# One head group's V on SyncE's queue in fp32, and the third keys in a buffer of raw keys: an attention and feed-forward kernel on one core

## The chip, the cores and the metric

The kernel runs on 1 core of one Trainium2 chip. The metric is device time in microseconds (us) of one execution; lower is better. TensorE (PE) multiplies matrices, VectorE (DVE) and ScalarE (ACT) work element by element, GpSimd (POOL) and SyncE (SP) here almost only issue DMAs. A DMA that POOL issues may change the type on its way (fp32 in HBM, fp16 in SBUF); POOL's transfers are the queue q0 of the profile ("software_dynamic"), SP's are q1 ("hardware_dynamic"). Both are moved by the same 16 DMA engines.

## What is computed

```
scores = scale * np.matmul(q, k.transpose(0, 1, 3, 2))      # q, k, v: 8 x 12 x 448 x 64, fp32
scores = scores - np.max(scores, axis=-1, keepdims=True)
attn = np.exp(scores)
attn = attn / (np.sum(attn, axis=-1, keepdims=True) + 1e-09)
attn_out = np.matmul(attn, v).astype(np.float32)

x = np.ascontiguousarray(attn_out.transpose(0, 2, 1, 3)).reshape(B * S, H * D)   # 3584 x 768
h = x @ w_in                                                # 768 x 2048
g = h * (1.0 / (1.0 + np.exp(-h)))
out = (g @ w_out).astype(np.float32)                        # 2048 x 768
```

Everything is read in fp32 and computed in fp16 with fp32 sums in PSUM.

## The kernel before

**Tiling.** A unit is one batch and one group of four heads (hg); there are 8 x 3 = 24 of them, numbered n = 3 x batch + hg. For each unit the raw keys and queries (128 partitions, 896 fp16 columns, 224 KB) are loaded, turned with 32 x 32 transposes on DVE (`turn_k`, L392, in three instructions or more; `turn_q`, L414), multiplied to scores on PE (`scores`, L471, matmuls at L460), and put through exp on ACT (`expo`, L501; L505 and L516, 128 x 896 at a time). PE then multiplies exp(scores) with ones, which gives the sums (part 0), and with V (parts 1 and 2, L568 for the first units), DVE turns the sums into reciprocals spread over the heads (`inverse`, L635: transpose L640, reciprocal L648, transpose L655), and multiplies the products with them into xT (`norm`, L666, L685). The feed-forward part (L697) follows batch by batch, mixed into the attention of later batches.

**The order of the work is written out ahead.** The program runs a planner (`Order`, L111) that keeps a clock for each engine, with a cost in us for each operation, and emits each engine's instructions in the order in which the planner would start them. Each engine then works through its own list strictly in that order; semaphores only make it wait. So a late operand of one instruction holds all that stands behind it on that engine. Waiting times of PE that the planner foresees are filled with matmuls of zeros (`run_zeros`, L2324, L2329); the first such stretch has `FIRST` = 47 blocks of 128 columns (L250, L2390).

**The first loads** stand in this order on POOL: keys and queries of unit 0 (the queries in two halves, `PIECES`), keys and queries of unit 1, keys of unit 2, V of batch 0, queries of unit 2, keys and queries of unit 3, then the first w_in pieces, and so on (L1216 to L1243). The semaphores of eight loads are used in turn, so a load waits for the eighth before it to land. Raw keys have a ring of two buffers ("rk", `NRK` = 2). The keys of unit 2, (batch 0, hg 2), are a guest: `GUEST` (L243) puts them not into that ring but into `room` (L344), the one of the two V buffers that batch 1 will use later, so that this load waits for nobody.

**V of batch 0** is one tile `VT[0]` (128 x 12 heads x 4 chunks x 64). `plan_v(0, 0, NG)` makes four loads of it, one for each 32 partitions, each for all 12 heads (192, 192, 144 and 144 KB; L361). `lift_v` (L369) on DVE then moves one half chunk of the second head group. PE's first product with V (unit 0, part 1) needs the four loads.

**What DVE does in the stretch in question**, in its order: keys of unit 1 (L407, L412, L407), queries of unit 1 (L424), keys of unit 2 (L407, L412, L407, out of `room`), sums of unit 0 (L640), `lift_v`'s copy (L372), reciprocal (L648), `lift_v`'s memset (L376), transpose back (L655), `norm` of unit 0, part 1 (L685), queries of unit 2 (L424), `norm` of part 2 (L685). PE's: scores of unit 0, unit 1's first scores, sums of unit 0, unit 1's second scores, V product part 1, unit 1's third scores, V product part 2, unit 2's first scores (which need unit 2's keys and queries turned).

Of the kernel before, what the change touches and what calls it, by code (L numbers as in the profile page):

```python
# [9 lines left out]
FP16 = mybir.dt.float16  # L10
FP32 = mybir.dt.float32
# [9 lines left out]
OVERLAP = {"ACT": 0.09, "DVE": 0.07}  # L21
DMA_LATE, DMA_MORE = 1.0, 0.6
LOADS, DMA_SLOW = 8, 1.45
DMA_ROW = 0.006
DMA_RATE = 13570.0
DMA_START = 1.2
# [84 lines left out]
class Order:  # L111
# [43 lines left out]
    def load(self, rows, row_bytes, emit, ring=None, gate=None):  # L155
        op = Op("POOL", 0.58, emit)
        self.pool.append((op, rows * (DMA_ROW + row_bytes / DMA_RATE) / 16, ring, gate))
        return op
# [56 lines left out]
def kernel(  # L215
# [9 lines left out]
    nc = tc.nc  # L225

    B, NH, S, D = q.shape
    DM = NH * D
    DFF = moe_w_in.shape[1]
    HG = 4  # L230
    NG = NH // HG
    TPP = S // 32
    NCH = 4
    X_TOK = {
        "low": ((0, 4), (4, 4), (8, 3), (11, 3)),
        "high": ((0, 3), (3, 3), (6, 4), (10, 4)),
    }
# [2 lines left out]
    NT = 2 * S // 128  # L240
    OH = DM // 2
    NRK, NRQ = 2, 4
    GUEST = (0, 2)  # L243
    PACE = 2.6
    BF0 = 4
    NPL = 4
    EAGER = 1
    HALVES = 0
    NEAR, LATE = 0.15, -0.3
    COLD, FIRST, QUIET = 8.5, 47, 0.16  # L250
    SHY = 0.5
    AWAIT = 1.0
    FAR = (NT * B // 4 - 1,)
# [27 lines left out]
    sb = ctx.enter_context(tc.tile_pool(name="sb", bufs=1))  # L281
# [36 lines left out]
    rawk, rawq, KT, QT, VT, E, T, acc, rdn_t, xT, g_t, ost_t = ({} for _ in range(12))  # L318
# [3 lines left out]
    def group_of(src, b, hg):  # L322
        return src[b, HG * hg : HG * (hg + 1)].rearrange("h (i g) d -> (h i) (g d)", g=TPP)

    def load_k(b, hg):
        if (b, hg) == GUEST:
            t = guest
        else:
            t = sb.tile([128, TPP * D], FP16, name=f"rk_{b}_{hg}", tag="rk", bufs=NRK)
        nc.gpsimd.dma_start(out=t, in_=group_of(k, b, hg))  # L330
        rawk[(b, hg)] = t

# [7 lines left out]
    def form(b, hg):  # L340
        return "low" if b == 0 else ("low", "high")[(NG * b + hg) % 2]


    room = sb.tile([128, NH, NCH, D], FP16, name="room", tag="V", bufs=2)  # L344
    guest = room.rearrange("p h c d -> p (h c d)")[:, 0 : TPP * D]

    def first_v():
        VT[0] = sb.tile([128, NH, NCH, D], FP16, name="V_0", tag="V", bufs=2)
# [2 lines left out]
    def load_v(b, hg0, hg1, x):  # L351
        if b not in VT:
            VT[b] = sb.tile([128, NH, NCH, D], FP16, name=f"V_{b}", tag="V", bufs=2)
        hs = slice(HG * hg0, HG * hg1)
        kind = form(b, hg0)
        if x == 0 and b > 0 and NG * b + hg0 < ALONE:
            lo = 64 if kind == "low" else 0
            nc.gpsimd.memset(VT[b][lo : lo + 64, hs, place(b, hg0, NCH - 1), :], 0.0)
        first, count = X_TOK[kind][x]
        at = int(kind == "high" and count < NCH)  # L360
        nc.gpsimd.dma_start(  # L361
            out=VT[b][32 * x : 32 * (x + 1), hs, at : at + count, :],
            in_=v[b, hs].rearrange("h (i g) d -> i h g d", g=TPP)[
                :, :, first : first + count, :
            ],
        )
# [25 lines left out]
    def turn_k(b, hg, c0=0, c1=NCH):  # L392
        t = rawk[(b, hg)][:].bitcast(FP32).rearrange("p (g i) -> p g i", i=32)
        if c0 == 0:
            kt = sb.tile([128, TPP, 32, 2], FP16, name=f"KT_{b}_{hg}", tag="KT", bufs=3)
            KT[(b, hg)] = kt
        kt = KT[(b, hg)]
        pairs = kt.rearrange("p g i e -> p (g i e)").bitcast(FP32)
        pairs = pairs.rearrange("p (g i) -> p g i", g=TPP)
        high = form(b, hg) == "high"  # L400
        full = pairs[:, 2 * high : 2 * high + 12].rearrange("p (c x) i -> p x c i", x=4)
        for x in (0, 2):
            first, count = X_TOK[form(b, hg)][x]
            toks = t[:, first : first + 2 * count].rearrange("p (x c) i -> p x c i", c=count)
            at = int(high and count == 4)
            c2 = min(c1, NCH - 1)
            nc.vector.transpose(  # L407
                out=full[:, x : x + 2, c0:c2], in_=toks[:, :, at + c0 : at + c2]
            )
            if count == 4 and c1 == NCH:  # L410
                lone = 12 * (not high)
                nc.vector.transpose(out=pairs[:, lone : lone + 2], in_=toks[:, :, 3 - 3 * at])  # L412

    def turn_q(n, g0, g1):  # L414
        t = rawq[n][:].bitcast(FP32).rearrange("p (g i) -> p g i", i=32)[:, g0:g1]
        if units[n][0] == B - 1:

            to = sb.tile([128, TPP * D], FP16, name=f"q_{n}", tag="rq", bufs=NRQ)
            nc.vector.transpose(
                out=to[:].bitcast(FP32).rearrange("p (i g) -> p g i", g=TPP), in_=t  # L420
            )
            rawq[n] = to
        else:
            nc.vector.transpose(out=t, in_=t)  # L424
        QT[n] = rawq[n].rearrange("p (q e) -> p e q", e=2)

    def score_banks(n, w, ys):
        for y in ys:
            third = n < NB0 and len(pS_t) % 3 == 2
            pS_t[(n, w, y)] = (early[0] if third else ps).tile(  # L430
                [128, 2, 512], FP32, name=f"s_{n}_{w}_{y}", tag="s", bufs=1 if third else 2
            )
# [22 lines left out]
    def place(b, hg, c):  # L455
        return (c + 1) % NCH if form(b, hg) == "high" else c
# [714 lines left out]
    od = Order(SHY)  # L1171
    s_ring, m_ring, e_ring = Ring(3), Banks((0, 1)), Banks(range(NE))
    rk_ring, rq_ring, v_ring = Ring(NRK), Ring(NRQ), Ring(2)
    kt_ring, t_ring = Ring(3), Ring(NT_)
    ld_k, ld_q, ld_v, ld_win, ld_wout, wout_rows = {}, {}, {}, {}, [], []
    kt_op, qt_op, exp_op, rdn_op, x_op, g_op = {}, {}, {}, {}, {}, {}

    def plan_k(b, hg):
        ring = None if (b, hg) == GUEST else rk_ring
        ld_k[(b, hg)] = od.load(128, 2 * D * TPP, lambda: load_k(b, hg), ring)  # L1180

    def plan_q(n):
        ld_q[n] = [
# [9 lines left out]
    def plan_v(b, hg0, hg1):  # L1193
        made = []
        for x in range(4):
            ring = v_ring if (x == 0 and hg0 == 0) else None
            heads, toks = HG * (hg1 - hg0), X_TOK[form(b, hg0)][x][1]
            made.append(
                od.load(32 * heads, 2 * D * toks, lambda x=x: load_v(b, hg0, hg1, x), ring)
            )  # L1200
        for hg in range(hg0, hg1):
            ld_v[(b, hg)] = made
# [9 lines left out]
    def plan_w_out(f0, f1):  # L1212
        wout_rows.append(f0)
        ld_wout.append(od.load(128 * (f1 - f0), 2 * DM, lambda: load_w_out(f0, f1)))

    plan_k(0, 0)  # L1216
    plan_q(0)
    plan_k(0, 1)
    plan_q(1)
    plan_k(0, 2)  # L1220
    plan_v(0, 0, NG)
    plan_q(2)
    plan_k(1, 0)
# [7 lines left out]
    plan_q(5)  # L1231
    plan_w_out(0, 4)
    plan_v(1, 0, 1)
    plan_w_out(4, 8)
    plan_w_out(8, 12)
    plan_v(1, 1, 2)
    plan_w_out(12, 16)
    plan_v(1, 2, 3)
    for n in range(NB0 + NG, NU):
        b, hg = units[n][:2]  # L1240
# [13 lines left out]
    def plan_turn(n):  # L1254
        b, hg, g0, g1 = units[n]
        if b == B - 1 and not rq_ring.can(1, od.now):
            return False
        if (b, hg) not in kt_op:
            if not kt_ring.can(1, od.now):
                return False  # L1260
            kt_ring.take()
            first = Op(
                "DVE", 0.73, lambda: turn_k(b, hg), [ld_k[(b, hg)]], 20,
                then=None if (b, hg) == GUEST else rk_ring.give,
            )
            if n == 0:
                first = Op("DVE", 0.4, lambda: turn_k(b, hg, 0, 2), [ld_k[(b, hg)]], 20)
            kt_op[(b, hg)] = od.add(first)
        if b == B - 1:
            rq_ring.take()  # L1270
        qt_op[n] = [
            od.add(
                Op(
                    "DVE",
                    0.13 + (g1 - g0) / 30.0,
                    lambda g0=g0, g1=g1: turn_q(n, g0, g1),
                    [load],
                    20,
                    then=rq_ring.give if b == B - 1 else None,
                )  # L1280
            )
            for load, (g0, g1) in zip(ld_q[n], PIECES if n == 0 else ((0, TPP),))
        ]
        if n == 0:
            rest_k.append(
                od.add(
                    Op(
                        "DVE",
                        0.45,
                        lambda: turn_k(b, hg, 2, NCH),  # L1290
                        [kt_op[(b, hg)], qt_op[0][0]],
                        20,
                        then=rk_ring.give,
                    )
                )
            )
        return True
# [3 lines left out]

    def leave_bank(name):
        return lambda at: m_ring.give(at, bank_of[name])

    lift = []
    for step, busy in ((0, 0.35), (1, 0.2)):
# [1030 lines left out]
    while True:  # L2337
# [47 lines left out]
        if warm["on"] and not dark and od.free["PE"] <= od.now and wait > QUIET and od.now > 0.9:  # L2385
            each = mm(128) if od.now > COLD else 0.107
            n = max(1, int((wait - 0.06) / each), int(wait / each + 0.9) * (od.now < COLD))
            wide = 4
            if warm.pop("first", None):
                n, wide = FIRST, 4  # L2390
# [36 lines left out]
```

## Time and profile before

| | us |
|---|---|
| median of three runs (lowest, highest) | 377.42 (377.36, 377.94) |
| the profiled execution, its own time | 377.82 |
| its span, first instruction to last | 376.0 |
| PE busy within the span, matmuls of zeros included | 370.4 |
| DVE busy | 292.4 |
| ACT busy | 255.6 |
| POOL busy (issuing DMAs and a few memsets) | 85.0 |

By stage, from the view of windows (busy us of each engine):

| stage, us from the start | length | PE | DVE | ACT | GB/s written by DMA |
|---|---|---|---|---|---|
| 1.0 to 6.0: loads on their way, zeros on PE | 5.0 | 5.00 | 2.07 | 1.02 | 95 |
| 6.0 to 17.5: unit 0 and most of unit 1 | 11.5 | 10.42 | 5.76 | 10.60 | 189 |
| 17.5 to 24.0: unit 1's end and unit 2 | 6.5 | 6.50 | 5.55 | 5.92 | 205 |
| 24.0 to 376.0: all the rest | 352.0 | 348.48 | 278.89 | 237.76 | 87 |

A line of the timeline view reads: start, length of the (merged) stretch, engine, source line, operation, written tile <- read tiles, shapes, count, and in brackets the idle time just before it with what ended it. Lines of the DMA view give, for the issues in a window, the destination and source, the issuing queue, the count, the size in KB as written, and the median us from issue to landing. In the view of the chain that ended last, a line is start, length, and what stood on that chain.

### The profile page before, as it was taken

Reading aid. Unit: us, or ns where it says so; the run is one execution under the profiler, and the core shown is the slowest. Engines: PE = TensorE matmul, PEld = TensorE weight load, DVE = VectorE, ACT = ScalarE, POOL = GpSimd, SP = SyncE. Lnnn points to the kernel's source line nnn. Section 1 sums busy time; section 2 is a strip of 40 time slices with the busy share of each in tenths; the row PEclk is TensorE's granted clock in tenths of the full one; section 3 lists DMA queues with packets and bytes.
Section 4 is the critical chain, followed back from the end, with each engine's and each line's share of the span. In section 5 each row is a group of like instructions: output and inputs, shape, how many; then the busy total and the mean of one; then the engine's idle time right before and its main releaser. Section 6 shows DMA issues by size and latency. Waiting matters only on the chain.

```text
span 376.0 us, 10031 instructions
## 1 busy us (share of the span) xinstructions
PE 370.4 (98%) x4052; PEld 189.3 (50%) x4052; DVE 292.4 (78%) x613; ACT 255.6 (68%) x402; POOL 85.0 (23%) x155
## 2 busy tenths in 40 slices
PE   8999999999999999999999999999999999999996
PEld 3365445444444444444444444545556765556774
DVE  3667958999995969995969998899579744648883
ACT  4988873887878788777878777658872238883121
POOL 7552437424016326006423200000000000000000
PEclk9999999999999999999999999999999999999999
DMA  7999999919049948147964421210001241000144
GB/s 112 198 208 210 206 204 183 199 18 135 14 99 137 171 51 120 30 94 106 171 97 57 60 53 45 53 34 0 0 3 46 63 107 39 0 3 26 50 115 150
DMA packets 35967, 34.49 MB, mean 92 GB/s; under 512 B 11856, under 2 KB 35152, under 8 KB 35920
## 3 DMA queue, kind: packets, MB, share of 16 engines
q0 software_dynamic: 25312, 22.82, 41.1%
q1 hardware_dynamic: 10064, 10.40, 10.2%
q8 instruction: 32, 0.52, 0.6%
q10 hardware_dynamic: 544, 0.62, 0.5%
q14 instruction: 15, 0.12, 0.1%
HBM read 45.61 MB, written 11.01 MB: 151 GB/s over the span
## 4 chain that ended last, share of the span: by engine, by line
PE 97%; DMA 1%; issue 0%; POOL 0%; DVE 0%; POOLq 0%
PE p L697 28%; PE h L697 21%; PE f L697 16%; PE s L460 12%; PE a L582 8%; PE o L697 3%; PE a L568 2%; PE n_Q L697 2%; PE a L615 2%; PE n_P L697 2%; DMA rq<-in_q_dram 1%; PE z L2329 1%; PE z L697 0%; PE z L568 0%; DVE ost L1033 0%
## 5 line engine op out<-in xcount | busy, mean ns | idle before, releaser
L516 ACT ACTIVATE E<-s 128x896 f16<-128x896 f32 x164 | 142.0, 919 | 24.8 <-PE s L460 24.7
L697 PE MATMUL h<-xT,w_in_t 128*32 128x448 f16 (+2 forms) x762 | 83.5, 348 | 0.0
L697 PEld LDWEIGHTS <-w_in_t 128*128 128x128 f16 (+1 forms) x909 | 54.6, 97 | 50.0 <-issue 8.1
L361 POOL DMA_DIRECT2D V<-in_v_dram x88 | 48.5, 565 | 49.7 <-PE a L582 29.2
L697 PEld LDWEIGHTS <-G 128*128 128x128 f16 (+1 forms) x652 | 40.1, 97 | 26.0 <-issue 5.0
L729 ACT ACTIVATE th<-h 128x448 f16<-128x448 f32 x67 | 36.6, 546 | 24.3 <-PE h L697 20.7
L697 PE MATMUL p<-w_out_t,G 128*128 128x384 f16 (+1 forms) x294 | 46.7, 327 | 0.0
L460 PE MATMUL s<-rq,KT 32*128 32x448 f16 (+3 forms) x728 | 44.9, 347 | 0.5 <-DVE rq L424 0.5
L697 PEld LDWEIGHTS <-S 128*128 128x128 f16 (+1 forms) x329 | 29.9, 98 | 21.3 <-issue 3.4
L773 DVE SCALAR_TENSOR_TENSOR G<-th,h 128x448 f16<-128x448 f16 (+1 forms) x64 | 35.7, 573 | 4.7 <-ACT th L729 4.3
L697 PE MATMUL p<-D,S 128*128 128x384 f16 (+1 forms) x217 | 39.3, 327 | 0.0
L1027 ACT COPY ost<-p 128x384 f32<-128x384 f32 x36 | 17.3, 480 | 26.8 <-PE p L697 24.2
L582 PE MATMUL a<-E,V 128*32 128x448 f16 (+1 forms) x640 | 32.7, 356 | 0.0
L685 DVE SCALAR_TENSOR_TENSOR xT<-a,rdn 128x448 f16<-128x448 f32 x46 | 26.9, 618 | 3.4 <-PE a L582 2.2
L338 POOL DMA_DIRECT2D rq<-in_q_dram x25 | 13.9, 558 | 67.0 <-PE s L460 58.2
L460 PEld LDWEIGHTS <-KT 32*128 32x128 f16 (+1 forms) x824 | 12.4, 96 | 31.0 <-issue 29.2
L529 DVE TENSOR_TENSOR T<-T,E 128x1792 f16<-128x1792 f16 x21 | 22.8, 1086 | 4.8 <-ACT E L516 4.8
L529 DVE TENSOR_TENSOR T<-E,E 128x1792 f16<-128x1792 f16 x21 | 22.7, 1082 | 4.1 <-ACT E L516 4.0
L901 DVE TENSOR_TENSOR p<-f,p 128x448 f32<-128x448 f32 x15 | 9.3, 623 | 20.3 <-PE f L697 13.9
L1049 DVE TENSOR_TENSOR ost<-p,ost 128x384 f32<-128x384 f32 x28 | 15.4, 552 | 12.2 <-ACT ost L1027 7.7
L697 PE MATMUL f<-sx,tw 128*128 128x448 f16 x102 | 23.7, 353 | 0.0
L582 PEld LDWEIGHTS <-V 128*32 128x32 f16 (+1 forms) x640 | 13.5, 95 | 18.0 <-issue 10.1
(140 smaller groups left out, 483.9 us busy)
## 6 DMA issues: line engine op xcount, KB each, us to landing
out_dram<-ost SPq DMA_DIRECT2D x146, 48.0 KB, 2.2
rk<-in_k_dram POOLq DMA_DIRECT2D x23, 224.0 KB, 5.3
rq<-in_q_dram POOLq DMA_DIRECT2D x23, 224.0 KB, 5.9
w_out_t<-in_moe_w_out_dram POOLq DMA_DIRECT2D x4, 768.0 KB, 12.6
V<-in_v_dram POOLq DMA_DIRECT2D x42, 64.0 KB, 4.4
out_dram<-wide SPq DMA_DIRECT2D x48, 48.0 KB, 1.6
V<-in_v_dram POOLq DMA_DIRECT2D x42, 48.0 KB, 4.6
w_in_t<-in_moe_w_in_dram POOLq DMA_DIRECT2D x6, 256.0 KB, 9.2
```

Source lines behind the costliest of these rows:

```text
L338: nc.gpsimd.dma_start(out=rawq[n][:, cols], in_=group_of(q, b, hg)[:, cols])
L361: nc.gpsimd.dma_start(out=VT[b][32 * x : 32 * (x + 1), hs, at : at + count, :], in_=v[b, hs].rearrange("h (i g) d -> i h g d", g=TPP)[:, : ...
L460: nc.tensor.matmul(out=pS[p0 : p0 + 32 * (x1 - x0), h % 2, at : at + q1 - q0], lhsT=KT[(b, hg)][32 * h : 32 * (h + 1), key_rows(b, hg, c, ...
L516: nc.scalar.activation(out=E[(n, w)][:, 2 * y : 2 * y + 2, :], in_=pS_t[(n, w, y)][:, :, 0:S], func=AF.Exp, scale=attn_scale,)
L529: nc.vector.tensor_tensor(out=T[n], in0=T[n] if step else E[(n, 0)], in1=E[(n, step + 1)], op=ALU.add,)
L582: nc.tensor.matmul(out=a[32 * h : 32 * (h + 1), 0:S], lhsT=VT[b][k0:k1, HG * hg + h, place(b, hg, c), part - 1 :: 2], rhs=e[k0:k1, h], sta ...
L685: nc.vector.scalar_tensor_tensor(out=x3(b, cc)[:, cc % 3, 32 * g0 : 32 * g1], in0=acc[(n, part)][:, 0:nq], scalar=0.5, in1=rdn_t[n].rearra ...
L697: nc.tensor.matmul(out=out[i : i + cut], lhsT=w[:, i : i + cut], rhs=x, start=start, stop=stop, skip_group_check=True,)
L729: nc.scalar.activation(out=th, in_=h_t[(b, f, t0)][:, 0:n], func=AF.Tanh)
L773: nc.vector.scalar_tensor_tensor(out=dst[:, f, at + lo : at + hi], in0=th_t[(b, f, t0)][:, lo - t0 : hi - t0], scalar=1.0, in1=h_t[(b, f, ...
L1027: nc.scalar.copy(out=ost(qd, *OUT[m]), in_=bank(qd, BANK[m]))
L1049: nc.vector.tensor_tensor(out=t, in0=bank(qd, BANK[m]), in1=t, op=ALU.add)
```

## The change

- V of head group 0 of batch 0 is no longer part of POOL's four loads, which now cover heads 4 to 11 alone. SP issues four DMAs for it (`raw_v`), in fp32 without a change of type, into the first half of `room`, seen as fp32. They are issued after a DVE memset of a few elements of that tile, which stands behind the transposes of unit 0's second half of queries. Two DVE copies (`cast_v`) then bring it to fp16 into `VT[0]`; in DVE's order they stand between the keys of unit 2 and the sums of unit 0. The planner is told that the data is there at 12.0 (`PLAIN`).
- The keys of unit 2 go into the ring of raw keys; `GUEST` is gone. The third load of keys so takes the buffer of the first.
- `FIRST` is 44 instead of 47.
- On all engines the order of the other instructions is as before; only the fill of zeros is cut differently in the first waits of PE. In the changed program the load of the third keys waits for DVE (the last transpose of unit 0's keys), and the first `cast_v` for SP's four DMAs.

```diff
+PLAIN = 12.0
...
-    GUEST = (0, 2)
...
-    COLD, FIRST, QUIET = 8.5, 47, 0.16
+    COLD, FIRST, QUIET = 8.5, 44, 0.16
...
     def load_k(b, hg):
-        if (b, hg) == GUEST:
-            t = guest
-        else:
-            t = sb.tile([128, TPP * D], FP16, name=f"rk_{b}_{hg}", tag="rk", bufs=NRK)
+        t = sb.tile([128, TPP * D], FP16, name=f"rk_{b}_{hg}", tag="rk", bufs=NRK)
         nc.gpsimd.dma_start(out=t, in_=group_of(k, b, hg))
         rawk[(b, hg)] = t
...
     room = sb.tile([128, NH, NCH, D], FP16, name="room", tag="V", bufs=2)
-    guest = room.rearrange("p h c d -> p (h c d)")[:, 0 : TPP * D]
+    v32 = room.rearrange("p h c d -> p (h c d)").bitcast(FP32)
+    v32 = v32[:, 0 : HG * NCH * D].rearrange("p (h c d) -> p h c d", h=HG, c=NCH)
+
+    def raw_v():
+        nc.vector.memset(v32[:, :, 0, 0:1], 0.0)
+        for x, (first, count) in enumerate(X_TOK["low"]):
+            nc.sync.dma_start(
+                out=v32[32 * x : 32 * (x + 1), :, 0:count, :],
+                in_=v[0, 0:HG].rearrange("h (i g) d -> i h g d", g=TPP)[
+                    :, :, first : first + count, :
+                ],
+            )
+
+    def cast_v(step):
+        rows, cs = ((128, slice(0, NCH - 1)), (64, slice(NCH - 1, NCH)))[step]
+        nc.vector.tensor_copy(out=VT[0][0:rows, 0:HG, cs], in_=v32[0:rows, :, cs])
...
         QT[n] = rawq[n].rearrange("p (q e) -> p e q", e=2)
+        if n == 0 and g0:
+            raw_v()
...
     def plan_k(b, hg):
-        ring = None if (b, hg) == GUEST else rk_ring
-        ld_k[(b, hg)] = od.load(128, 2 * D * TPP, lambda: load_k(b, hg), ring)
+        ld_k[(b, hg)] = od.load(128, 2 * D * TPP, lambda: load_k(b, hg), rk_ring)
...
             made.append(
-                od.load(32 * heads, 2 * D * toks, lambda x=x: load_v(b, hg0, hg1, x), ring)
+                od.load(
+                    32 * heads,
+                    2 * D * toks,
+                    lambda x=x: load_v(b, max(hg0, int(b == 0)), hg1, x),
+                    ring,
+                )
             )
...
             first = Op(
-                "DVE", 0.73, lambda: turn_k(b, hg), [ld_k[(b, hg)]], 20,
-                then=None if (b, hg) == GUEST else rk_ring.give,
+                "DVE", 0.73, lambda: turn_k(b, hg), [ld_k[(b, hg)]], 20, then=rk_ring.give
             )
...
+    here = Op("SP", 0.0, None)
+    here.done = PLAIN
+    for step, busy in ((0, 0.95), (1, 0.4)):
+        od.add(Op("DVE", busy, lambda step=step: cast_v(step), [here], 20))
```

## The prediction

> **What bounds the kernel now.** I read the page's busy times and chain first, to see which engine sets the end:
>
> ```profile
> PE 370.4 (98%) x4052; PEld 189.3 (50%) x4052; DVE 292.4 (78%) x613; ACT 255.6 (68%) x402; POOL 85.0 (23%) x155
> ...
> PE 97%; DMA 1%; issue 0%; POOL 0%; DVE 0%; POOLq 0%
> ```
>
> PE sets it, and the chain enters PE early. So a change of the first microseconds counts by how much later or earlier PE's unbroken stretch begins. Next the chain of 0 to 35 us, about the first use of V:
>
> ```profile
> 13.93 0.75 PE s L460 x8
> 14.68 0.57 issue
> 15.25 0.94 PE a L568 x16
> 16.19 0.51 PE s L460 x7
> 16.70 0.87 PE a L568 x16
> 17.57 0.70 PE s L460 x16
> 18.27 1.63 PE a L568 x32
> ```
>
> PE stands still for 0.57 until 15.25, where its first product with V starts; behind that I see no gap. The windows agree: PE is busy 6.50 of the 6.50 us from 17.5 to 24.0 and 348.48 of the 352.0 after. Third, DVE's timeline over the same stretch, since PE's scores of unit 2 (17.50 in PE's timeline) need its transposes:
>
> ```profile
> 11.68 0.38 DVE L407 STREAM_TRANSPOSE KT<-room 128x192 f32<-128x192 f32 x1 [1.08 <-DMA room<-in_k_dram]
> ...
> 13.98 0.65 DVE L640 STREAM_TRANSPOSE rdn<-z 128x448 f32<-128x448 f32 x1 [1.53 <-PE z L568]
> 14.66 0.22 DVE L372 COPY V<-V 64x256 f16<-64x256 f16 x1
> ...
> 15.21 0.62 DVE L655 STREAM_TRANSPOSE rdn<-inv 128x448 f32<-128x448 f32 x1
> 16.24 0.62 DVE L685 SCALAR_TENSOR_TENSOR xT<-a,rdn 128x448 f16<-128x448 f32 x1 [0.41 <-PE a L568]
> 16.78 0.63 DVE L424 STREAM_TRANSPOSE rq<-rq 128x448 f32<-128x448 f32 x1
> ```
>
> DVE is idle for 1.53 before L640 at 13.98 and for 0.41 before L685 at 16.24. The transposes of unit 2's queries stand behind L685 and end at 17.41, just ahead of the scores. Last, how long DMAs take:
>
> ```profile
> L361 POOL DMA_DIRECT2D V<-in_v_dram x4: 672/676/687, 4.6 to 6.4; - x4
> DMA to landing us min/median/max: 7.9/8.4/8.8
> ```
>
> V's last load, issued at 6.4, lands at 6.4 + 8.8 = 15.2. That is what PE waited for. With it I read a stretch in which POOL's and SP's queues are both in use, and one in which SP's is alone:
>
> ```profile
> 184.27 0.59 POOL L338 DMA_DIRECT2D rq<-in_q_dram  x1
> ...
> rq<-in_q_dram POOLq DMA_DIRECT2D x1, 224.0 KB, 6.5
> ...
> 185.40 0.31 SPq L1020 DMA_DIRECT2D out_dram<-ost  x1
> ...
> out_dram<-ost SPq DMA_DIRECT2D x1, 48.0 KB, 5.6
> ...
> out_dram<-ost SPq DMA_DIRECT2D x1, 48.0 KB, 1.5
> ```
>
> POOL's load of 184.27 lands at 190.8. SP's small store, issued 1.13 later, lands at 191.0. The store issued at 101.73, with nothing before it, took 1.5 (last line). So an SP transfer is served about where its issue time puts it among POOL's loads; having a queue of its own does not let it pass them.
>
> **The change part by part.**
>
> *Zeros, 44 for 47.* The first stretch takes 5.11 us for 47 blocks from 1.00, 0.109 each, so it ends at 5.78 instead of 6.11. The first scores wait for the first half of unit 0's queries (DVE 5.42 + 0.41 = 5.83) and may start 0.15 to 0.2 earlier. The next scores, at 7.67, wait for the second half, which lands at 7.2 (the chain has that DMA from 2.48 for 4.71); nothing here moves it. Value 0, both bounds 0.1; without that cover it would be a gain of 0.2.
>
> *Third keys in the ring.* The load can now be issued when DVE has turned the last of unit 0's keys, 6.01 + 0.20 = 6.21; from such a wait's end to the issue it is 0.28 (keys turned from 11.68, the next POOL load issued at 11.94), so at 6.5 instead of 4.04. V's four follow to about 8.9 instead of 6.4, then queries of unit 2 at 9.5 (7.47 before), keys of unit 3 at 10.0 (9.40), queries of unit 3 at 10.6 (10.22). The next, w_in at 11.94, waits for the third keys' landing as before. What covers this is the queue: loads issued from 4.6 to 7.5 land 7.9 to 8.8 later. The load ahead, queries of unit 1, lands at 9.9, and the very first load of the same size took 3.5 from issue to landing in an empty queue: 6.5 + 3.5 = 10.0, before the 11.66 of now. Value 0. If the queue does run dry, the row to go by is the key load issued at 3.0, which took 5.8 with three loads ahead of it: 12.3, so 0.6 late; the transposes would end at 13.1, still ahead of SP's data, and the outer bound of the sum stays as below.
>
> *The memset* (0.07, as other small DVE memsets) ends at 7.7, in DVE's idle 7.62 to 8.86: 0.
>
> *SP's four DMAs.* Issued at 7.9 to 9.2 (SP's four stores from 101.73 take 1.71). POOL's V loads are issued at 7.05, 7.6, 8.2 and 8.8, so the two sets are interleaved in line. From the third keys' landing (11.66) to V's last (15.2) it was 3.5 us for 12 heads; the same data must come in now. In line by issue, SP's last has all of it before it except perhaps POOL's last piece, 0.6: landing 14.5 to 15.2. Outer bound: behind the queries of unit 2 too (15.7). I take 14.9.
>
> *The two copies on DVE*, 768 and 256 elements a partition, fp32 to fp16. No row has one. Fp16 copies of 1024 and 256 elements take 0.417 and 0.220, that is 0.154 + 0.257 ns per element; so 0.35 + 0.22 = 0.57 at the least. At one element a cycle, as L685 works (448 in 0.62), 0.95 + 0.42 = 1.37. I take the fp16 slope doubled, for twice the bytes read: 0.55 + 0.29 = 0.84. By the Trainium skill ("VectorE: DVE Perf Modes", the perf-mode tier table) an fp32 copy within SBUF runs at two elements a cycle, which as an estimate gives 0.84 too; if it means the same source and destination type only, the sum is 0.5 more.
>
> *Where the stall goes.* The copies stand before L640. They are free until 13.98 plus L685's idle 0.41 = 14.39. With the data at 14.9 they end at 15.77. L640 to L655 take 1.85 (13.98 to 15.83), so L685 starts at 17.62; the queries of unit 2 behind it are turned by 17.62 + 1.17 = 18.79 (17.41 before). PE: the V product starts at 15.8 instead of 15.25, third scores and part 2 follow to 18.1, and then PE waits for the queries until 18.88 instead of 17.50. ACT cannot cover it: its four exps from 16.73 last 3.35 and the next need those scores. So +1.38. Since PE has hardly an idle spot behind 17.5 (3.5 us in 358, part of it at the very end), I let it pass whole to the end.
>
> Sum: 377.82 + 1.38 = 379.2 for the profiled execution. That one lies 0.40 above the median 377.42, so the median is predicted at 378.8. With the inner bounds (14.5 and 0.57: +0.68) and the outer ones (15.7 and 1.37: +2.68) the forecast's own range is 378.1 to 380.1.
>
> **Rivals.**
>
> *A. The two queues take turns at equal shares.* SP's data is a third of V, 1.17 us of the engines' time; at half the share from 8.9 (7.9 + 1.0) it is in at 11.3 to 12. The third keys are then pushed back by the same 1.17, to 12.83, and are turned by 13.6, with the copies behind them: done at 14.45, against the free 14.39: +0.06. With the copies' bounds -0.2 to +0.6, and with equal counts of packets, of which POOL's are the larger here (1,792 bytes of a row of keys against 1,024 and 768), SP's last piece may come at about 14.1: +0.6, with the slow copies +1.1. Time 377.5, from 377.2 to 378.5. For it speaks only that the queues are separate; against it the pair of rows at 184 to 191. A page of the Trainium skill does say this ("DMA: Bandwidth & Descriptors", Queues, rings and completion order: each engine goes round-robin between its queues, a packet at a time); by it the time would be 377.5, and the trace does not agree.
>
> *B. The other side, not slower: SP's transfers fill what POOL's leave.* DMA writes 166 GB/s at 6 to 9 and 186 at 9 to 12, against 205 after 15, so there is room for (39 + 19) x 3 / 205 = 0.85 us of work. If SP's four land by 12.2 with the third keys still at 11.66, the copies run 12.45 to 13.3 in the idle 1.53, PE's V product starts at 14.7, L685 at 15.83: a gain of 0.41, 377.0. It decides at a landing of 13.5: before it a gain, after it a loss. More is possible only if ACT's idle 0.25 and 0.50 for scores (16.48 and 20.08) go too, another 0.75: 376.3. Against it: the same rows at 184 to 191, though there the queue was as full. By the skill's rules for kernel authors on that DMA page, issuing from several engines brings no bandwidth, which speaks against B; the trace has no run that shows it.
>
> **Chances.** A measurement of this kernel can tell about 0.2% (0.75 us) from no change. Forecast 0.60 (nearly all of it slower by more than that), A 0.22 (0.07 slower, 0.15 within), B 0.18 (0.05 within, 0.13 faster). Slower 0.67, within 0.20, faster 0.13. The range is 376.9 to 380.1: all of the forecast, all of A, and B's plain gain; left out are B's larger gain and a landing after 15.7. The likeliest case's own range is 378.1 to 380.1.
>
> **What would show it.** Forecast: the first copy starts at 14.5 to 15.7 after a wait for SP's DMAs, L640 at 15.4 to 16.5, scores of unit 2 at 18.2 to 20, and ACT idle for over a microsecond before them. A: third keys' transposes start at 12.8 rather than 11.7 and the copies follow at once. B: copies from 12.5, L640 still at 13.98. Copies of 0.35 or 0.95 show the slope wrong. Third keys after 12 with SP's data later still would show the queue run dry. If the scores of unit 2 are late but the end is not, my step that PE cannot catch up is wrong.

## The result, and the profile after

The changed kernel takes 379.69 us in the median of six executions (379.23 to 381.53), the kernel before 377.42 beside it: the ratio is 1.0064, interval 1.0049 to 1.0080. That is slower by 2.27, and inside the predicted 376.9 to 380.1, above the single value 378.8. The profiled execution is the longest of the six: 381.53, its span 379.6 (before: 377.82 and 376.0). So its times lie about 1.8 above the median's, and sizes are compared by runs further down. The same kernel run again (experiment 10) has a median of 381.10, 3.47 above the kernel before beside it, and that is outside the range.

The page of the changed kernel first, engines' busy times and the chain by engine:

```profile
PE 370.8 (98%) x4051; PEld 189.3 (50%) x4051; DVE 292.9 (77%) x616; ACT 255.9 (67%) x402; POOL 84.8 (22%) x155
...
PE 94%; DMA 3%; DVE 0%; ACT 0%; SPq 0%; POOL 0%; issue 0%; DVEq 0%; POOLq 0%
```

PE is busy for 0.4 longer in a span that is 3.6 longer, and DMA has 3% of the chain instead of 1%: PE was kept waiting. Where, the chain of the first 35 us tells (start, length, what):

```profile
2.46 5.55 DMA rq<-in_q_dram
...
8.45 0.04 DVE room L346
...
9.88 6.61 DMA room<-in_v_dram
16.50 0.03 issue
...
16.62 0.57 DVE V L357
17.19 0.04 issue
17.23 0.94 PE a L582 x16
...
18.87 1.71 ACT E L530 x2
```

Two DMAs in line: the second half of unit 0's queries (landed at 8.01) holds the transposes ahead of the memset, so the last of SP's four loads goes out only at 9.88; that lands at 16.50, and 0.12 later DVE can copy. (ACT's two exps at the end are looked at below, under "The stall's way".) DVE's timeline shows who stands behind (the lines of the changed file are 12 to 14 higher: L654 is L640 of before, L699 is L685, L436 is L424):

```profile
8.04 0.41 DVE L436 STREAM_TRANSPOSE rq<-rq 128x224 f32<-128x224 f32 x1 [1.58 <-DMA rq<-in_q_dram]
8.41 0.06 DVE L346 MEMSET room<- 128x4 f32 x1
...
12.20 0.38 DVE L419 STREAM_TRANSPOSE KT<-rk 128x192 f32<-128x192 f32 x1 [0.99 <-DMA rk<-in_k_dram]
...
16.62 0.84 DVE L357 CAST V<-room 128x768 f16<-128x768 f32 x2 [3.66 <-DMA room<-in_v_dram]
17.39 0.63 DVE L654 STREAM_TRANSPOSE rdn<-z 128x448 f32<-128x448 f32 x1
...
19.33 0.62 DVE L699 SCALAR_TENSOR_TENSOR xT<-a,rdn 128x448 f16<-128x448 f32 x1
19.88 0.64 DVE L436 STREAM_TRANSPOSE rq<-rq 128x448 f32<-128x448 f32 x1
```

DVE stands idle for 3.66 before the copies; the sums start at 17.39 (13.98 before), and unit 2's queries are turned at 20.52 (17.41 before). PE's timeline at that place, before and after:

```profile
15.25 0.56 PE L568 MATMUL a<-T,V 128*32 128x448 f16 x8 [0.57 <-issue]
...
17.50 0.77 PE L460 MATMUL s<-rq,KT 32*128 32x224 f16 x16
```

```profile
17.23 0.56 PE L582 MATMUL a<-T,V 128*32 128x448 f16 x8 [1.73 <-DVE V L357]
...
20.57 0.93 PE L474 MATMUL s<-rq,KT 32*128 32x224 f16 x16
```

PE's idle time before the first product with V grew from 0.57 to 1.73, and the scores of unit 2 start at 20.57 instead of 17.50, 3.07 later. Last, the DMA view of the issues from 8.4 to 9.95 (destination and source, queue, count, KB each, median us to landing):

```profile
room<-in_v_dram SPq DMA_DIRECT2D x2, 128.0 KB, 5.6
rq<-in_q_dram POOLq DMA_DIRECT2D x1, 224.0 KB, 7.2
V<-in_v_dram POOLq DMA_DIRECT2D x2, 96.0 KB, 7.2
room<-in_v_dram SPq DMA_DIRECT2D x2, 96.0 KB, 6.5
```

SP's loads take 5.6 to 6.5 where POOL's take 7.2: a little shorter. Taken singly, SP's first (issued 8.50) landed at 14.1, ahead of POOL's load of 8.44, which landed at 15.4; SP's last (9.88), on which the copies wait, landed at 16.50, in the midst of POOL's loads of 9.01 and 9.57 (16.4 and 16.7). What the two queues moved meanwhile stands under rival A.

### The profile page after: what moved, and what is told of

Its sections match the earlier page's. It is cut to its first block, busy times and chain, and to the rows that moved or that the text cites. A ratio compares the mean times of both kernels' runs of the same rounds, so it can differ in the third digit from the quotient of the medians.

```text
span 379.6 us, 10043 instructions
## 1 busy us (share of the span) xinstructions
PE 370.8 (98%) x4051; PEld 189.3 (50%) x4051; DVE 292.9 (77%) x616; ACT 255.9 (67%) x402; POOL 84.8 (22%) x155
## 4 chain that ended last, share of the span: by engine, by line
PE 94%; DMA 3%; DVE 0%; ACT 0%; SPq 0%; POOL 0%; issue 0%; DVEq 0%; POOLq 0%
PE p L711 28%; PE h L711 21%; PE f L711 16%; PE s L474 11%; PE a L596 8%; PE o L711 3%; PE a L582 2%; PE n_Q L711 2%; PE a L629 2%; DMA room<-in_v_dram 2%; PE n_P L711 2%; DMA rq<-in_q_dram 1%; ACT E L530 0%; SPq L348 0%; PE z L711 0%
## 5 line engine op out<-in xcount | busy, mean ns | idle before, releaser
L699 DVE SCALAR_TENSOR_TENSOR xT<-a,rdn 128x448 f16<-128x448 f32 x46 | 26.9, 618 | 2.7 <-PE a L596 2.1
L915 DVE TENSOR_TENSOR p<-f,p 128x448 f32<-128x448 f32 x15 | 9.3, 623 | 20.3 <-PE f L711 13.9
L1063 DVE TENSOR_TENSOR ost<-p,ost 128x384 f32<-128x384 f32 x28 | 15.5, 552 | 12.2 <-ACT ost L1041 7.7
L596 PEld LDWEIGHTS <-V 128*32 128x32 f16 (+1 forms) x640 | 13.5, 95 | 18.1 <-issue 11.0
```

What stands on the lines that cost most here:

```text
L596: nc.tensor.matmul(out=a[32 * h : 32 * (h + 1), 0:S], lhsT=VT[b][k0:k1, HG * hg + h, place(b, hg, c), part - 1 :: 2], rhs=e[k0:k1, h], sta ...
L699: nc.vector.scalar_tensor_tensor(out=x3(b, cc)[:, cc % 3, 32 * g0 : 32 * g1], in0=acc[(n, part)][:, 0:nq], scalar=0.5, in1=rdn_t[n].rearra ...
L1063: nc.vector.tensor_tensor(out=t, in0=bank(qd, BANK[m]), in1=t, op=ALU.add)
```

## The experiments

The kernel before ran beside every one of them: 377.72 in the median beside the first four, 377.82 beside the next four, 377.63 beside the last two. All times are medians.

**1. The zeros undone: 47 blocks again.**

```diff
-    COLD, FIRST, QUIET = 8.5, 44, 0.16
+    COLD, FIRST, QUIET = 8.5, 47, 0.16
```

> The changed kernel with the first stretch of zeros at 47 blocks again. Theory (in line): the cost is V's place in the line of DMAs and DVE's order behind it, so the zeros are worth nothing: 379.2 to 380.0, within 0.3 us of the changed kernel, copies of V starting at 15.5 to 16.7. Rival (zeros): the shorter stretch lets PE's clock or the first scores come wrong; then this is back at 377.4 to 377.9.

Measured: 379.68 (379.42 to 382.09), ratio 1.0045 (1.0032 to 1.0058). The three blocks bring nothing that can be told from the scatter of the changed kernel itself. The time is as expected, the copies are not (17.18 instead of 15.5 to 16.7). In this profile the queries' second half landed at 8.55, SP's loads went out at 9.04 to 10.43, the copies started at 17.18 and the scores of unit 2 at 21.13: the latest of all.

**2. The third keys in the ring, alone** (the kernel before, with only `GUEST` taken away).

```diff
-    GUEST = (0, 2)
...
-        ring = None if (b, hg) == GUEST else rk_ring
-        ld_k[(b, hg)] = od.load(128, 2 * D * TPP, lambda: load_k(b, hg), ring)
+        ld_k[(b, hg)] = od.load(128, 2 * D * TPP, lambda: load_k(b, hg), rk_ring)
...
```

> The kernel before with one part of the change: the third keys go into the ring of raw keys, V stays with POOL in fp16. Theory (in line): the queue hides the later issue (6.5 instead of 4.0); third keys land at 11.7 to 12.3, V's last at 15.2 to 15.7, time 377.3 to 377.9. Rival (keys): the load that waits for DVE pushes every load behind it, and that is the loss: V's last at 16 or later, time 379 or more.

Measured: 378.22 (377.80 to 380.39), ratio 1.0018 (1.0005 to 1.0031). That is half a microsecond slower in the median and 0.2 to 1.2 by the interval, just above the expected 377.3 to 377.9. In its profile the keys are turned from 10.83 (11.68 before), unit 2's scores start at 17.41, and the span is 376.0 as before, so the trace names no place for the 0.5 in the median.

**3. The third keys as a guest again, behind the fp32 V in the same idle buffer** (the changed kernel else).

```diff
+    GUEST = (0, 2)
...
+    guest = room.rearrange("p h c d -> p (h c d)")[:, 2 * HG * NCH * D : 2 * HG * NCH * D + TPP * D]
...
```

> The changed kernel with the third keys a guest again, in the half of the idle V buffer that the fp32 V leaves free, so that POOL's loads go out as early as before. Theory (in line): SP's DMAs, still issued from about 7.9, now stand behind all of POOL's V loads (issued by 6.9) and perhaps behind the queries of unit 2: they land at 15.3 to 16.5, and the time is no better than the changed kernel's, 379.0 to 380.0. Rival (keys): with the keys early again the loss is gone, 377.4 to 377.8.

Measured: 381.89 (381.09 to 384.49), ratio 1.0110 (1.0087 to 1.0134): above the changed kernel's 1.0064, and above the expected 379.0 to 380.0. POOL no longer waits for DVE, so all its V loads go out at 4.55 to 6.3, ahead of SP's four (7.06 to 8.48). SP's first still landed at 12.5, ahead of POOL's last two V loads (14.2 and 14.8); SP's last lands at 16.0, only 0.5 earlier though it was issued 1.4 earlier than in the changed kernel. DVE's timeline:

```profile
16.13 1.00 DVE L362 CAST V<-room 128x768 f16<-128x768 f32 x2 [4.99 <-DMA room<-in_v_dram]
```

So the ring, for all that its load is later, seems to have helped this change: it held POOL's V back and let SP's into the line.

**4. SP's loads called behind the first key transposes,** not behind the queries' second half; they go out at 5.44 to 6.84.

```diff
     def turn_k(b, hg, c0=0, c1=NCH):
...
+        if (b, hg) == (0, 0) and c0 == 0:
+            raw_v()
...
     def turn_q(n, g0, g1):
...
-        if n == 0 and g0:
-            raw_v()
```

> The changed kernel with SP's four DMAs issued after the first transposes of unit 0's keys, at about 5.4 to 7.0 instead of 8.5 to 10.3; nothing else is moved. Theory (in line): they stand ahead of the third keys (issued at 6.5 to 6.75), land by 11.5 to 12.5, the third keys at 12.8 to 13.5; the copies run behind the keys' transposes and end at 14.4 to 15.2, L640's counterpart starts there, time 377.4 to 378.3. Rival (slow queue): SP's queue gets only a small share beside POOL's, whatever its place; V still lands at 15 or later, time 379 or more. Rival (keys): the third keys are no earlier, so 379 or more as well.

Measured: 378.39 (377.58 to 379.63), ratio 1.0014 (1.0001 to 1.0027). The last of SP's lands at 12.3, the copies run from 12.70 in DVE's idle time, the scores of unit 2 start at 17.05, 0.45 ahead of the kernel before. TensorE keeps that lead until 192 us, where it loses 0.8 in one place (last section). So the median is not the gain that the opening promised: it lies just above the expected 378.3, and the interval just clear of 1.

**5. The memset, and with it SP's loads, ahead of the transposes of the queries' second half and not behind them:** one instruction moved past one.

```diff
     def turn_q(n, g0, g1):
+        if n == 0 and g0:
+            raw_v()
         t = rawq[n][:].bitcast(FP32).rearrange("p (g i) -> p g i", i=32)[:, g0:g1]
...
-        if n == 0 and g0:
-            raw_v()
```

> The changed kernel, but the memset of V's fp32 buffer, and with it SyncE's four loads, stand ahead of VectorE's transposes of the second half of unit 0's queries and not behind them. Theory (SyncE's loads are served by issue time in line with GpSimd's; in the changed kernel they went out at 8.5 to 9.9 because the memset waited for the queries' second half, and every microsecond of their landing past 14.4 is lost to the end): issued at about 6.5 to 8.0, among GpSimd's V loads instead of behind them, last landing 13.5 to 15.0, the copies end 14.4 to 15.8, scores of unit 2 start 17.5 to 18.9, time 377.7 to 379.0, so 0.7 to 2.0 under the changed kernel. Rival (the landing is late because the fp32 pieces are slow in themselves, or because SyncE's queue waits until GpSimd's has run dry): landing stays at 16 to 16.5 and the time at 379.3 to 379.9.

Measured: 378.04 (377.52 to 379.44), ratio 1.0012 (0.9999 to 1.0024). DVE's timeline:

```profile
6.13 0.06 DVE L346 MEMSET room<- 128x4 f32 x1
6.43 0.41 DVE L438 STREAM_TRANSPOSE rq<-rq 128x224 f32<-128x224 f32 x1 [0.24 <-DMA rq<-in_q_dram]
...
12.62 0.80 DVE L357 CAST V<-room 128x768 f16<-128x768 f32 x2 [0.78 <-DMA room<-in_v_dram]
13.77 0.65 DVE L654 STREAM_TRANSPOSE rdn<-z 128x448 f32<-128x448 f32 x1 [0.35 <-PE z L582]
```

SP's four go out at 6.22 to 7.61, the last lands at 12.5, the copies are done before the sums are there (L654 waits for PE, no longer for them), and most of the loss is gone: 0.22 is left against the kernel before beside it. The rival (the fp32 pieces are slow in themselves, or SP waits until POOL's queue is empty) falls: POOL's fourth V load, issued 1.1 behind SP's last, landed at 14.1.

**6. The planner told of the late V** (16.5 instead of 12.0; unit 0's products with V wait for the copies, which stand behind the sums' transposes).

```diff
-PLAIN = 12.0
+PLAIN = 16.5
...
-    for step, busy in ((0, 0.95), (1, 0.4)):
-        od.add(Op("DVE", busy, lambda step=step: cast_v(step), [here], 20))
+    casts = [
+        od.add(Op("DVE", busy, lambda step=step: cast_v(step), [here], -20))
+        for step, busy in ((0, 0.55), (1, 0.3))
+    ]
...
+            if n == 0:
+                deps += casts
```

> The changed kernel, with the planner told that the raw V is there at 16.5 instead of 12.0 and that the first products with V wait for the copies, which then stand on VectorE behind the row sums' transposes that stood behind them. Theory (what is lost is what VectorE's fixed order puts behind the late copies: row sums, xT, the turning of unit 2's queries): the row sums' chain runs from 14 on, TensorE has other products to do while V is late, and the time is 377.7 to 378.7. Rival (V's lateness itself stops TensorE, in whatever order, since unit 0's and 1's later work all needs V): V's products start at 17.4 as in the changed kernel and the time stays at 379.3 to 380.

Measured: 380.82 (379.69 to 381.50), ratio 1.0080 (1.0066 to 1.0095). Neither theory held. The opening is mended: the sums' transposes run at 13.97 again and the scores of unit 2 start at 17.43, with SP's last landing at 15.6. But a new plan orders everything else anew too, and PE pays later. Its timeline, 15 us on:

```profile
29.95 0.54 PE L711 MATMUL h<-xT,w_in_t 128*128 128x224 f16 x4 [0.34 <-DVE G L778]
31.68 0.54 PE L711 MATMUL h<-xT,w_in_t 128*128 128x224 f16 x4 [1.19 <-DVE xT L688]
```

DVE had stood idle for 3.53 there for a load of keys that POOL could issue only at 18.2. These 1.53, and 1.19 more of idle PE in the first 20 us, account for the 2.6 by which PE ends later than before. So the order on DVE was what carried the late V to unit 2's scores; that a plan made for the late V is cheaper is not shown.

**7. Experiments 3 and 4 together:** the guest, and SP's loads early.

> The version with SyncE's loads called behind the first key transposes (378.4), and with the third keys loaded early again, into the part of V's idle buffer that the fp32 V leaves free. Theory (loads are served in line by issue time): third keys land at 10 to 11.5 instead of 12.0, SyncE's V 0.5 to 1.5 later than the 12.3 of that version, so at 12.8 to 13.8, still before 14.4; V by GpSimd about where it was; time 377.3 to 378.4, a gain only if unit 1's or unit 2's scores were waiting for the third keys. Rival (the room taken in line matters as in the late version, where the guest cost 2 us): SyncE's V lands after 15 and the time is 378.5 to 380.

Measured: 378.82 (378.15 to 379.92), ratio 1.0033 (1.0021 to 1.0046). SP's last was issued at 6.83, as in experiment 4, but has POOL's keys and V before it: landing 13.9 instead of 12.3, the copies from 13.99, the scores of unit 2 at 17.89. Landing and time lie just above the expected 12.8 to 13.8 and 377.3 to 378.4. Against experiment 4 the guest costs 0.7 by the ratios, whose intervals overlap, and a good deal less than 2 us.

**8. The first group's V early without SP and without copies:** the kernel before, POOL's V loads split.

```diff
-    plan_v(0, 0, NG)
+    plan_v(0, 0, 1)
+    plan_v(0, 1, NG)
```

> The kernel before, with GpSimd's loads of the first batch's V split: the four of head group 0 first, then four of the other eight heads, all in fp16; nothing by SyncE and nothing to cast. It asks whether the first group's V early is worth anything when it costs no copy. Theory (VectorE's copies and SyncE's late landing make the loss; TensorE's 0.57 of idle at 15.25 is all there is to win): head group 0's V lands at 13.5 to 14.2 and not 15.1, but four more issues of 0.57 push queries of unit 2 and keys of unit 3 back by 2.3, whose landing is not waited for; time 377.2 to 377.9. Rival (GpSimd's issue time is the scarce thing at the start): the loads behind are late, unit 2's scores wait for the queries' landing, time 378.3 to 379.5.

Measured: 379.82 (378.90 to 381.78), ratio 1.0064 (1.0044 to 1.0084); missed by two microseconds. The first group's V lands at 11.7 and PE starts on it at 13.83 instead of 15.25, yet unit 2's scores start at 17.80, later than before: the planner, reckoning with eight issues, put both products of `norm` ahead of the queries' transposes on DVE. This order is new everywhere, so the run does not price the four issues by themselves. It shows that 1.4 earlier at the first product with V need not move the end.

**9. Zeros on TensorE where it waits for V** (the changed kernel else), and **10. the changed kernel again,** on the same chip.

```diff
         if part == 0 and n == ADDED:
             made = [(0, None, 0, 0, S)] + [x for x in made if x[0] == NCH - 1]
+        if (n, part) == (0, 1):
+            for _ in range(6):
+                nc.tensor.matmul(
+                    out=a[:, 0:S],
+                    lhsT=zeros,
+                    rhs=zeros[:, 0:1].to_broadcast([128, S]),
+                    start=True,
+                    stop=True,
+                )
```

> The changed kernel with six blocks of zeros (448 columns, about 1.15 us together) on TensorE right before its first product with V, where it stood still for 1.73 us in the changed kernel's profile; they are written to the bank that this product starts anew. Theory (the loss has two parts: V is late by about 2, and in some executions the idle stretch of 1.3 to 2.2 us lets the granted clock fall to 0.5 for 3.4 us, which costs another 1.1): the granted clock stays 1.00 from 16 to 24 us, the first product with V starts when the copy is done as before, and the time is 378.9 to 379.5 in all runs, with none above 380.3. Rival (the low clock follows from something else at that time, or costs nothing since TensorE then waits for other engines anyway): the clock falls to 0.5 all the same, or the time stays at 379.5 to 380 with runs above 380.5.

> The changed kernel once more, to stand beside the version with zeros on the same chip. Theory: 379.3 to 380 in the median, runs spread from 379.2 to 381.5, those with an average clock of 0.996 or less at 380.5 and more. Rival (runs spread for other reasons): clock and time have nothing to do with each other.

Measured: with zeros 380.35 (379.18 to 382.05), ratio 1.0079 (1.0055 to 1.0103); again without 381.10 (379.56 to 382.88), ratio 1.0084 (1.0060 to 1.0109). The average granted clock was 0.998 to 1.000 in all six executions with zeros, and 0.991, 0.994 and 0.995 in three of the six without. So the low clock goes; but the expectations of 378.9 to 379.5 with zeros, of no time above 380.3 (380.74, 381.58 and 382.05 were) and of 379.3 to 380 without failed, and the two intervals overlap. The executions without zeros and with a low clock were all above 380.5, as expected. The clock is a small part of the spread. The profiled execution with zeros (379.18) happened to have an early landing, 14.78, nearly the forecast's 14.9. DVE's and PE's timelines of it:

```profile
14.90 0.79 DVE L357 CAST V<-room 128x768 f16<-128x768 f32 x2 [2.48 <-DMA room<-in_v_dram]
...
18.11 0.64 DVE L436 STREAM_TRANSPOSE rq<-rq 128x448 f32<-128x448 f32 x1
```

```profile
14.93 1.32 PE L578 MATMUL a<-zeros 128*128 128x448 f16 x6
16.18 0.56 PE L591 MATMUL a<-T,V 128*32 128x448 f16 x8
...
18.80 0.58 PE L474 MATMUL s<-rq,KT 32*128 32x224 f16 x16 [0.30 <-DVE rq L436]
```

Scores of unit 2 at 18.80, 1.30 later than before, and a span of 377.4, 1.4 longer.

**Side by side.** Nine profiled executions, in the order of the start of the copies (us; times from DVE's, SP's and PE's timelines):

| version | SP's four issued | copies start | scores of unit 2 | span |
|---|---|---|---|---|
| before | - | - | 17.50 | 376.0 |
| 5: memset ahead | 6.22 to 7.61 | 12.62 | 17.05 | 375.7 |
| 4: behind the first keys | 5.44 to 6.84 | 12.70 | 17.05 | 376.5 |
| 7: the same, with guest | 5.17 to 6.83 | 13.99 | 17.89 | 376.4 |
| 9: with zeros | 6.91 to 8.31 | 14.90 | 18.80 | 377.4 |
| 3: guest | 7.06 to 8.48 | 16.13 | 20.60 | 379.3 |
| 10: changed, again | 7.28 to 8.68 | 16.21 | 20.67 | 379.2 |
| changed | 8.50 to 9.88 | 16.62 | 20.57 | 379.6 |
| 1: 47 zeros | 9.04 to 10.43 | 17.18 | 21.13 | 380.2 |

From 13.99 on the scores start 3.90 to 3.95 behind the copies (4.46 or so in 3 and 10, where PE, at half clock, was behind DVE), and the span follows them: from 18.80 to 21.13 is 2.33 in the scores and 2.8 in the span. By that distance a start at 13.5 would give 17.45, about the 17.50 of the kernel before.

No version beats the kernel before. Experiments 4 and 5 come within its scatter; where PE's lead of 0.45 goes is seen in one execution of 4 alone.

## Why the prediction was right, and where its sizes were off

Way and mechanism were right: SP's data late, the copies ahead of the sums in DVE's order, the queries of unit 2 behind them, PE waiting for those. That the time came into the range is in part luck. The range ends at 380.1, which is a landing at 15.7 together with slow copies of 1.37; the copies took 0.84, and a landing after 15.7, which the range leaves out, was seen in three of four profiles of this order (16.1, 16.5, 17.1). The six executions of the result have a median span of about 378, which by the table above, as an estimate, goes with copies at about 15.3; the repeat's median of 381.10 is outside.

**Zeros, value 0:** right, as experiment 1 shows.

**Third keys, value 0:** near, but not shown to be nothing: alone they cost 0.5 (0.2 to 1.2). They were issued at 6.75 (6.5 predicted), their transposes moved from 11.68 to 12.20 in the changed kernel and forward to 10.83 in experiment 2; DVE waited for V after them in any case. The written sign of a queue run dry, third keys after 12 with SP's data later still, is there in the changed kernel (12.17 and 16.50; DMA wrote 157 GB/s from 8 to 11, 184 before). But in experiments 1 and 10 the third keys landed at 11.8 and 10.2, and SP's data at 17.1 and 16.1 all the same; so it is not what made V late.

**The memset, 0, ending at 7.7:** its own 0.06 is nothing, but as a gate it was mis-sized. It stands behind a transfer whose landing changes from execution to execution: the queries' second half landed between 6.40 and 8.55 in the profiles above, SP's first issue 0.5 behind it, wherever the memset stood behind that transfer. Experiment 5 takes this gate away, and 0.22 is left of the loss (378.04 against the 377.82 of its own kernel before), where the changed kernel lost 2.27 and, repeated, 3.47. The gate is not the whole of it: in experiment 10 SP's loads went out at 7.3, earlier than the forecast's 7.9, and the last landed at 16.1. Between experiments 5 and 9 the last issue differs by 0.7 and its landing by 2.3; why this is so steep stays open.

**SP's last landing, 14.9 (14.5 to 15.2, outer bound 15.7):** the term that was mis-sized most. It came at 14.8 in one profile of this order, and at 16.1, 16.5 and 17.1 in the others. The wait from the last issue was 6.5 to 7.4, where the forecast had 5.7. The doubtful words of the forecast are "the same data must come in now". In bytes written it is not the same: POOL's V was 672 KB in fp16, now it is 448 KB by POOL and, by the DMA view above, 448 KB by SP in fp32. The 224 KB more are 1.0 to 1.1 us at the 208 to 228 GB/s that the windows show from 11 to 16.5; added to 14.9 they give 16.0. That written bytes were what limited is argued from these rates; no run changed the bytes alone. Nor can the bytes be all: experiment 9 moved the same ones and had its last landing at 14.78. Why one and the same order lands anywhere from 14.8 to 17.1 is open.

**The two copies, 0.55 + 0.29 = 0.84:** right; 0.84 in the changed kernel (the first 0.57), 0.79 to 1.00 over all versions. (The lower bound of the sum, +0.68, and the upper, +2.68, leave out the 0.03 from landing to first copy that the single value has.)

**The stall's way (sums, `norm`, queries of unit 2, scores):** right to a tenth in its length. The forecast had 3.98 from the copies' data to the scores (14.9 to 18.88); measured 3.90 to 3.95 from the copies' start. Experiment 9 is the forecast's own case: data at 14.78, scores at 18.80, span +1.4 where +1.38 was written. Experiment 6, with another order on DVE, has scores at 17.43 although the data comes at 15.6. By the written signs, experiment 9's 14.90, 15.62 and 18.80 (copies, sums, scores) lie within; the changed kernel's profiled execution lies above all three (16.62, 17.39, 20.57).

The chain of the changed kernel names ACT's two exps, and not DVE, before these scores: the second exp ends at 20.58, the queries' transposes at 20.52. Which one the scores wait for, experiment 9 tells. ACT's timeline of it:

```profile
18.48 0.91 ACT L530 ACTIVATE E<-s 128x896 f16<-128x896 f32 x1
```

There the scores start at 18.80, 0.05 behind the queries, while this exp runs until 19.39. So they need the queries; that ACT ends at the same moment in the changed kernel is then a coincidence.

**Passed whole to the end:** right. After unit 2's scores PE hardly waits again in the changed kernel, and its instructions lie 3.38 behind from 22 us to the end. The 0.3 above the 3.07 of the scores is a low clock, which the forecast did not have.

**Rival A (queues take turns)** did not come in landing or time: the third keys were not followed at once by the copies, and SP's last landed near the end of the line. In the changed kernel SP's four, issued from 8.50 to 9.88, landed at 14.1, 14.6, 15.7 and 16.5; POOL's loads issued at 8.44, 9.01 and 9.57 landed at 15.4, 16.4 and 16.7. But its mechanism is not refuted. The DMA view of the changed kernel, from 8 to 11 us and from 11 to 14 (packets, MB, share of 16 engines; q0 is POOL's queue, q1 SP's):

```profile
q0 software_dynamic: 545, 0.47, 109.3%
q1 hardware_dynamic: 4, 0.00, 0.5%
```

```profile
q0 software_dynamic: 685, 0.29, 81.3%
q1 hardware_dynamic: 421, 0.35, 44.7%
```

For some 2.3 us after the first issue SP's queue moved next to nothing while POOL's moved 0.47 MB; then the two queues ran side by side, and SP's wrote more than POOL's. What A had wrong is the start (8.9) and the bytes (a third of V instead of 448 KB); why SP's share falls again after 14 (0.10 MB of 0.55 until 16.5) is open. So early SP loads do pass: in experiment 3 SP's first landed ahead of three POOL loads that were issued 0.2 to 1.3 before it. The last one, on which the copies wait, mostly did not: in eight of nine profiles it landed behind every POOL load issued more than 0.35 before it. In experiment 7 it passed two, issued 0.5 and 1.1 before (13.9 against 14.7 and 14.3). Issued 2.3 earlier (experiment 5), it landed 4.0 earlier, with two of POOL's V loads before it in line, and not all four and unit 2's queries too.

**Rival B (a gain, if landed before 13.5)** did not occur in the changed kernel. Its point of decision, a landing at 13.5, is bracketed: at 13.9 scores come 0.4 late, at 12.5 they come 0.45 early. But the early scores brought no gain in the median of experiments 4 and 5.

## What to carry to other kernels

A second DMA queue did not bring its whole load in ahead of the first one's backlog: early loads passed some of it, but the last, for which the consumer waits, landed about where its issue time put it. So look at when the issue instruction runs, how many bytes stand before it, and what it waits for; here a memset of 0.06 us, put on the wrong side of a late transfer, cost most of the 2.3 us (with it moved, 0.2 is left). Count a load that drops its type change in the bytes that it writes (argued here, not shown alone), and when an order is written out ahead, price the first wait on an engine by everything queued behind it.

## What the runs showed that was not expected

**After some short waits TensorE's granted clock is half.** The view of windows, changed kernel (columns: length, PE, PEld, DVE, ACT, POOL busy, granted clock, DMA share, GB/s):

```profile
17.00:18.00 1.00, 0.77 (x16) 0.34 (x16) 1.00 (x3) 0.31 (x1) 1.00 (x2) 1.00 1.11 192
18.00:19.00 1.00, 1.00 (x16) 0.26 (x16) 0.94 (x5) 0.15 (x1) 0.61 (x2) 0.70 1.23 201
19.00:20.00 1.00, 1.00 (x16) 0.33 (x8) 0.89 (x3) 1.00 (x2) 0.33 (x1) 0.50 1.23 204
20.00:21.00 1.00, 0.87 (x20) 0.37 (x16) 1.00 (x2) 0.58 (x1) 0.70 (x2) 0.50 1.24 206
21.00:22.00 1.00, 1.00 (x24) 0.34 (x20) 1.00 (x5) 0.47 (x1) 0.40 (x2) 0.60 1.24 205
22.00:23.00 1.00, 1.00 (x28) 0.49 (x20) 0.72 (x2) 1.00 (x2) 0.52 (x1) 1.00 1.24 204
```

After PE's idle 1.73 the granted clock is 0.5 for some 3.4 us (0.6, 2.0 and 0.8 of these rows, as an estimate); eight products with V take 0.94 there instead of 0.56. The same followed idle times of 2.29 (experiment 10), 2.37 (experiment 3) and 1.74 (experiment 1, ending at 17.80), and not 0.96 (experiment 7). The length of the wait alone does not decide: in experiment 1 an idle time of 1.90, ending at 9.04, left the clock at 1.00. What else decides is not shown. Much of it hides behind DVE, which is late anyway: 0.3 reached the end here, 0.5 in experiment 10. With zeros in the gap the same windows of experiment 9 show 1.00. The Trainium skill ("TensorE: Matmul & The Clock Gate", Part 1: The HAM clock gate) says that half rate follows an idle window of about 3.4 us and lasts until a busy one of that length has passed; the half rate and its length agree with this trace, but an idle time of half that length was enough here.

**Two waits of TensorE that no semaphore explains.** PE's timeline of experiment 4:

```profile
191.57 0.56 PE L474 MATMUL s<-rq,KT 32*128 32x448 f16 x5
192.56 0.37 PE L474 MATMUL s<-rq,KT 32*128 32x448 f16 x3 [0.43 <-issue]
```

In the midst of eight matmuls of one kind PE waits 0.43 for nothing that the profile shows ("issue"). The DMA view has, for 190.0 to 191.2 of this run, one packet of 16 KB on a queue of instructions:

```profile
q8 instruction: 1, 0.02, 4.9%
```

It starts at 190.16, when 4,970 of PE's matmuls and weight loads had started, and ends at 191.10, 1.46 before PE goes on; in the other versions the packet of this stretch came earlier in PE's work, after 4,786 to 4,922. Experiment 8 has the one other such wait (0.43, ending at 26.29), 1.30 after the end of a packet that came late too: after 658 of PE's matmuls and weight loads, after 576 to 626 in the other versions. That the late packet caused the wait is read from this agreement; it was not tried. The Trainium skill ("Runtime: NRT & Kernel Launch", Instruction fetch mechanics) says that an engine fetches its instructions by DMA of its own in blocks of 16 KiB, mostly hidden; the packet's size agrees, and these two places may be where it was not hidden.
